# A scan-and-feed-forward kernel on one core: the late part of `a` loaded and scanned later, and the first steps put in another order

## The chip, the core and the metric

The kernel runs on one core of one Trainium2 chip. The metric is the device time of a run in microseconds. Five engines take part: TensorE (PE, with its weight loads as PEld), VectorE (DVE), ScalarE (ACT), GpSimd (POOL) and SyncE (SP, which here only issues transfers). ACT and POOL issue transfers too.

## The reference

```python
# attention-like part: 4 batches, 8 heads, 768 positions in chunks of 32, D = 32, N = 16
cum = np.cumsum(log_a[chunk]);  L = exp(cum[i] - cum[j]) for j <= i
y = (C B^T * L) x + (C state) * exp(cum)
state = exp(sum(log_a)) * state + sum_j B x * exp(cum[-1] - cum)
# feed-forward part, on the 3072 rows of 256 values that y gives
out = relu(y @ w_in) ** 2 @ w_out          # w_in 256 x 2048, w_out 2048 x 256
```

What the decay needs of `a` is the running product of `a` within chunks; everything else is products of matrices.

## The kernel before, in words

The positions are cut into 12 **units** of 256 rows: four batches for each third `j` of the sequence (units 0 to 3 have `j` = 0, units 4 to 7 `j` = 1, units 8 to 11 `j` = 2). A unit's first half makes its part of y (the tile `T`), its second half, the **block** of the same number, is the feed-forward part. In a block there are eight pairs of 128 hidden columns. For each pair, four matmuls with `w_in` (`mm1`, L390) fill one bank of PSUM, ACT evicts it with a relu into `hb` (L395), DVE squares it into `h` (L401), and four matmuls with `w_out` (`mm2`, L417) add it to the block's output.

Nothing schedules this at run time. The string `ORDER` is a list of steps, and each engine carries out its own instructions strictly in the order in which the steps stand. A step is a short token:

- `a0` to `a7` are the `mm1` steps of block 0 with their evictions, `b0` to `b7` those of block 1, and so on to `l`; `A0` to `L7` are the `mm2` steps; `qa0` squares what `a0` left. `a5@6` means that the step writes PSUM bank 6.
- `fa0`, `fa1` load the first third of `a` (32 rows of 128 values each, L117, tile `a_nat64`), and `la` loads the **late part** of it, the other two thirds (128 rows of 128 values, L544, tile `a_nat128`). `ldB1:s` loads B of unit 1 on SP's queue, `:a` stands for ACT's, and `:h`, `:l` for halves by head. `wi0` to `wi3` and `wo0` to `wo3` load quarters of `w_in` and `w_out` on POOL's queue (L141, L145).
- `sk` clips and scans the first third of `a` on DVE (L455, L456, tile `cp64`); `sp` turns it into P, the running products with positions on partitions, by small fp32 matmuls (L439). `sn` is the scan of the late part (`cp128`), `p` its matmuls (L439 again, eight of them, with a copy by ACT into `P_sb`, L525), `pn` a small product by DVE (`pick_p128`, L520), and `pt` two matmuls with it (L529, with a copy by ACT into `Ptot`, L530). Only units 4 to 11, and the carry from the first third to the second, need what the late part gives.
- For a unit: `pc`, `pb`, `px` scale or cast its C, B and x (`px` is L179); `tr` transposes on PE, `tc` copies the result; `mt` makes the scores (L222); `mk` masks a quarter of the scores directly on DVE (L231), `sc` copies a quarter by ACT and `ms` masks the copy (L240, on POOL or DVE); `u` and `in` are the products with x (L247), `ca` the carried state; `t` copies the finished `T` out of PSUM; `us`, `sf`, `za`, `zb`, `sa`, `sb` make the state for the next chunk (`zb` is L322 or L317 on DVE, `sb` is L333 on POOL).
- `id3:512@5` is three **filler** matmuls of 512 columns on constants (L463). They compute nothing and wait for nothing but their bank.

Transfers issued by SP and ACT share eight completion semaphores in turn, so each such transfer is issued only when the one eight places ahead of it in the program has landed.

Steps from unit 6 on (`rg6` and later) follow a regular pattern, in which PE always has a next step at hand.

Of the kernel before, what the change touches and what calls it, by code (L numbers as in the profile page):

```python
# [30 lines left out]
def kernel(  # L31
# [22 lines left out]
        us1 a3@7 qa2 b0@5 jz2:p qa1 b2@4 qa3 qa0 b3@6 pb2:a b1@2 qb0 ldB3:s ldC3:s pc2:v wo1 qb1 qb2 a4@7 a5@0 wi3
        b4@3 qa5 tr2@41 B0 A0 tc2:1:a iv:32:64 iv:16:32 qb3 qa4 tc2:0:a b5@5 zb1 B1 A1 mt2 B2 ldx3:s B3 A3 sc2 A2 qb4
        qb5 mk2 mk2 b7@0 wo2 ms2:v sb1 mk2 qb7 a6@5 a7@4 pb3:a wo3 px2 ld4 b6@2 A4 A5 pc3:v qa6 u2@45 ina2 inb2 tr3@31
        B5 B4 zb0 sb0 qa7 ld6 sf2 tc3:1:v qb6 pc4:p tc3:0:a ca2 pb4:p px3:v pq t2:aa us2 A6 mt3 u3@45 mk3 us3 A7 mk3
        tr4 c0@4 za3 mk3 ld5 c6@0 c5@7 B6 sa3 mk3 pc5:p afC2 pb5 c1@2 ld7 qc0 px5:p px4:v qc1 zb2 qc6 qc5 c2@4 B7 c7@1
# [679 lines left out]
```

## Time and profile before

| what | us |
|---|---|
| median of the 3 timed runs | 115.52 |
| lowest and highest of them | 115.5, 116.46 |
| profiled execution, span from first to last instruction | 114.5 |
| PE busy in it | 108.4 |
| DVE, ACT, POOL busy | 86.0, 76.6, 47.7 |

The profile is of one execution of its own; its span is 1.02 us below the median of the timed runs, which count what lies around the span as well. PE's busy time contains fillers, and it counts overlapping ends of matmuls, so a busy PE need not be doing useful work at its best rate. For that, the starts of the matmuls in the trace are the better guide.

### The profile page before, as it was taken

To read this page: it belongs to the slowest core of one execution; us is meant where nothing else is said; L and a number is where in the kernel's file an instruction comes from. 1 tells how busy PE (TensorE), PEld (TensorE's weight loads), DVE (VectorE), ACT (ScalarE), POOL (GpSimd) and SP (SyncE) were. 2 spreads that over 40 slices of the span, in tenths; PEclk is the share of its full clock that TensorE was granted. 3 is DMA by queue.
4 is the path that set the end of the run, shared out by engine and by line. 5 is a ranking of instruction groups with operands and counts; after the bars stand their busy time and mean duration, and the time that the engine had idled before them with its cause. 6 is when DMAs were issued, how large, how long until landed. Compare 5 with 4: busy or idle time off the path is not lost.

```text
span 114.5 us, 4010 instructions
## 1 busy us (share of the span) xinstructions
PE 108.4 (95%) x1629; PEld 93.8 (82%) x1630; DVE 86.0 (75%) x193; ACT 76.6 (67%) x160; POOL 47.7 (42%) x97
## 2 busy tenths in 40 slices
...
GB/s 25 204 184 165 201 188 218 214 171 175 140 166 193 86 250 105 162 95 155 156 121 134 127 97 149 104 121 51 0 98 68 0 100 0 17 80 0 92 0 92
DMA packets 47814, 13.46 MB, mean 118 GB/s; under 512 B 44276, under 2 KB 45876, under 8 KB 47796
## 3 DMA queue, kind: packets, MB, share of 16 engines
...
q0 software_dynamic: 1664, 2.10, 11.1%
q10 hardware_dynamic: 2304, 0.48, 2.0%
...
q14 instruction: 6, 0.05, 0.1%
HBM read 10.58 MB, written 3.15 MB: 120 GB/s over the span
## 4 chain that ended last, share of the span: by engine, by line
PE 77%; DMA 8%; DVE 5%; ACT 4%; issue 1%; POOL 1%; ACTq 1%; POOLq 0%
PE pp L417 33%; PE pp L390 33%; PE pp L247 7%; DMA w_out_b<-in_moe_w_out_dram 5%; PE pp L222 3%; DMA B_nat<-in_B_dram 3%; ACT hb L395 2%; DVE mts L240 1%; DVE h L401 1%; PE pp L463 1%; ACT jt L170 1%; DVE Pinv L537 1%; DVE mts L231 1%; ACT T L210 1%; POOL Sd L333 1%
## 5 line engine op out<-in xcount | busy, mean ns | idle before, releaser
L395 ACT ACTIVATE hb<-pp 128x512 bf16<-128x512 f32 x96 | 54.9, 600 | 22.5 <-PE pp L390 20.7
L401 DVE TENSOR_TENSOR h<-hb 128x512 bf16<-128x512 bf16 x96 | 44.9, 487 | 12.7 <-ACT hb L395 12.4
L417 PE MATMUL pp<-w_out_b,h 128*128 128x256 bf16 (+1 forms) x400 | 54.0, 268 | 0.1
L390 PE MATMUL pp<-T,w_in_b 128*128 128x256 bf16 x384 | 53.5, 273 | 0.1
L390 PEld LDWEIGHTS <-w_in_b 128*128 128x128 bf16 x384 | 41.5, 114 | 2.1 <-issue 0.8
L417 PEld LDWEIGHTS <-h 128*128 128x128 bf16 x400 | 37.5, 98 | 4.7 <-issue 0.9
L231 DVE TENSOR_TENSOR mts<-pp,mask 128x512 bf16<-128x512 f32 x45 | 29.7, 679 | 1.6 <-PE pp L222 1.6
L333 POOL TENSOR_TENSOR Sd<-z,Pquad 128x256 bf16<-128x256 f32 x16 | 11.0, 695 | 34.7 <-DVE z L317 22.8
L179 POOL TENSOR_TENSOR xs<-x_nat,Pinv 128x256 bf16<-128x256 f32 (+1 forms) x17 | 13.3, 800 | 2.3 <-DMA x_nat<-in_x_dram 2.2
L160 POOL TENSOR_TENSOR jt<-C_nat,P_sb 128x128 bf16<-128x128 f32 x18 | 7.9, 457 | 4.7 <-DMA C_nat<-in_C_dram 4.7
L463 PE MATMUL pp<-const-bfloat16-1.0 128*128 128x512 bf16 (+2 forms) x25 | 6.8, 427 | 1.0 <-PEq L722 0.8
L317 DVE SCALAR_TENSOR_TENSOR z<-z,Ptot,us 128x64 f32<-128x64 f32 x8 | 2.9, 356 | 5.4 <-ACT us L301 5.4
L247 PE MATMUL pp<-mts,xs 64*32 64x128 bf16 x384 | 6.1, 219 | 0.8 <-DVE mts L240 0.8
L424 ACT COPY osb<-pp 128x512 f32<-128x512 f32 x11 | 6.4, 584 | 0.5 <-PE pp L417 0.4
L172 POOL CAST jt<-B_nat 128x128 bf16<-128x128 f32 x17 | 5.5, 352 | 1.7 <-DMA B_nat<-in_B_dram 1.7
L463 PEld LDWEIGHTS <-const-bfloat16-1.0 128*128 128x128 bf16 x26 | 2.7, 116 | 3.9 <-issue 3.5
L222 PE MATMUL pp<-bct 32*64 32x256 bf16 x192 | 5.1, 280 | 0.5 <-DVE bct L212 0.5
L247 PEld LDWEIGHTS <-xs 64*32 64x32 bf16 x384 | 4.2, 90 | 1.2 <-issue 1.1
L284 ACT CAST T<-pp 128x512 bf16<-128x512 f32 x7 | 4.1, 585 | 1.6 <-PE pp L247 1.4
L210 ACT CAST T<-pp 128x256 bf16<-128x256 f32 x8 | 2.7, 375 | 2.4 <-PE pp L247 2.3
L247 PE MATMUL pp<-bct,Sd 128*128 128x128 bf16 x40 | 4.2, 220 | 0.0
...
## 6 DMA issues: line engine op xcount, KB each, us to landing
x_nat<-in_x_dram SPq DMA_DIRECT2D x11, 256.0 KB, 3.6
out_dram<-osb SPq DMA_DIRECT2D x11, 256.0 KB, 3.0
B_nat<-in_B_dram SPq DMA_DIRECT2D x11, 128.0 KB, 3.0
C_nat<-in_C_dram SPq DMA_DIRECT2D x11, 128.0 KB, 4.2
w_in_b<-in_moe_w_in_dram POOLq DMA_DIRECT2D x4, 256.0 KB, 6.6
w_out_b<-in_moe_w_out_dram POOLq DMA_DIRECT2D x4, 256.0 KB, 6.7
x_nat<-in_x_dram ACTq DMA_DIRECT2D x2, 128.0 KB, 3.5
bct<-jt SPq DMA_TRANSPOSE x8, 3.2
```

The lines of the kernel that those rows point to most:

```text
L160: eng.tensor_tensor(out=_fap(jt[k % 3], 128 + 144 * g, [[384, 2], [32, 4], [1, 16]]), in0=_fap(loaded[k]["C"], 128 * g, [[16, 2], [32, 4], ...
L179: eng.tensor_tensor(out=_fap(xs, 256 * r, [[256, 2 // n], [32, 8], [1, 32]]), in0=_fap(loaded[k]["x"], 32 * r, [[32, 2 // n], [64, 8], [1, ...
L222: nc.tensor.matmul(pp[64 * u:64 * u + 64, q, r * 256:r * 256 + 256], bct[32 * q:32 * q + 32, r, 0, u * 64:u * 64 + 64], _fap(bct[32 * q:32 ...
L231: nc.vector.tensor_tensor(out=live[k]["mts"][:, q].rearrange("p r g i -> p (r g i)"), in0=pp[:, q, :], in1=mask, op=ALU.mult)
L247: nc.tensor.matmul(dst, w, v, start=bool(need), stop=False, skip_group_check=True, **({} if pos is None else {"tile_position": pos}))
L333: nc.gpsimd.tensor_tensor(out=_fap(S_d, 0, [[128, 2], [32, 4], [1, 32]]), in0=_fap(z, 0, [[32, 2], [0, 4], [1, 32]]), in1=_fap(Pquad, 4 * ...
L390: nc.tensor.matmul(pp[:, h, i * 256:(i + 1) * 256], _fap(w, g * w.shape[2] + (o // 2) * 512 + 2 * (o % 2) + i, [[4, 128]]), T[blk][:, g].r ...
L395: nc.scalar.activation(out=hb.rearrange("p i t -> p (i t)"), in_=pp[:, h, :], func=AF.Relu)
L401: nc.vector.tensor_tensor(out=h2, in0=hb, in1=hb, op=ALU.mult)
L417: nc.tensor.matmul(dst, h2[:, i, r * 128:(r + 1) * 128], w_out_b[gi][:, 2 * o + i, c0:c1], start=first, stop=(fp == 7 and i == 1), skip_gr ...
L424: nc.scalar.copy(out=osb, in_=pp[:, 6 if blk == 1 else 7, :])
L463: nc.tensor.matmul(pp[:, h, 0:int(cols)], ones_b[:, 0:128], ones_b[:, 0:int(cols)] if dep is None else dep, start=True, stop=True, skip_gr ...
```

## The change

Only the string `ORDER` differs, and in it only the steps up to the sixth unit (to about `D0` and `e0`). The late part of `a` (`la`) moves from second place in the list to a place behind the loads of units 0 and 1; its scan (`sn`), its matmuls (`p`, `pt`) and its small product (`pn`) move behind the first `mm1` steps of blocks 0 and 1. Around that, most steps of the first six units stand in another order, some change engine (`px0` goes from POOL to DVE, `pbh0` from ACT to POOL), `mm1` and `mm2` steps of blocks 0 to 3 are exchanged among themselves, and the fillers have other numbers and sizes. The computation is the same. The core of the diff:

```diff
-        id3:512@5 fa1:a la fa0:s ku ef ldx0:h:a eb id2:512@5 ti id1:512@5 gB3 pi ldB0:l:a hd ldC0:l:a ldB0:h:s
...
-        mk1 mk1 px1:p mk1 t0:aa p2@0 a1@5 id3:128@0 a0@4 u1@12 mk1 ldC2:s ina1 inb1 pn sf1 a2@3 ca1 pt@6 t1:vv ldx2:s
...
+        jz1:v ti pi ku ldx0:h:a ldC0:h:s fa1:a ef ldC0:l:a mb hd gB3 fa0:s ldB0:l:a id2:256@3 ldx0:l:a ldB0:h:s eb
...
+        inb1 pb2:a a2@0 sf1 wo1 ca1 ldx2:s t1:vv ldB3:s a3@4 qa0 wi3 us1 sn1 qa2 qa1 b0@5 b1@7 qa3 b2@1 qb2 p2@5 pc2:p
+        qb0 pn pt@5 a5@6 ldC3:s qb1 b3@3 b4@2 qb4 a4@0 tr2@41 iv:32:64 B0 qb3 wo2 tc2:1:a B1 A0 tc2:0:v b5@2 zb1 B2 B3
```

**SP's queue at the start.** These are the first transfers that SP issues; `a_nat128` is the late part of `a`, `a_nat64` the first third, the digit in `B_nat1` is the unit. Before:

```order
L544 DMA a_nat128_98<-in_a_dram 128x1x128
L117 DMA a_nat64_97<-in_a_dram 32x128
L127 DMA B_nat0_146<-in_B_dram 128x4x32
L127 DMA C_nat0_149<-in_C_dram 128x4x32
L127 DMA B_nat1_159<-in_B_dram 128x8x32
L127 DMA C_nat1_177<-in_C_dram 128x8x32
L127 DMA x_nat1_270<-in_x_dram 128x8x64
```

And with the change:

```order
L127 DMA C_nat0_134<-in_C_dram 128x4x32
L117 DMA a_nat64_97<-in_a_dram 32x128
L127 DMA B_nat0_144<-in_B_dram 128x4x32
L127 DMA B_nat1_159<-in_B_dram 128x8x32
L127 DMA C_nat1_163<-in_C_dram 128x8x32
L127 DMA x_nat1_184<-in_x_dram 128x8x64
L544 DMA a_nat128_98<-in_a_dram 128x1x128
```

The late part went from first to seventh place, and a half of C of unit 0 stands first instead.

**PE around the matmuls of the late part.** Before, the eight matmuls of `p` (L439) stood between unit 0's carried state (`Sd0_0`) and block 0's first `mm1` step:

```order
L247 LDWEIGHTS Sd0_0_267
L247 MATMUL pp_120<-bct0_191,Sd0_0_267 128x128
L439 MATMUL pp_120<-eye_f_88,cp128_102 64x64 x4
L390 LDWEIGHTS w_in_b0_112
L390 MATMUL pp_120<-T0_334,w_in_b0_112 128x256
```

and `pt` (L529) stood between unit 1's carried state and the fourth `mm1` step of block 0. Now both stand next to each other, behind the `mm1` steps `b0`, `b1`, `b2` of block 1 (the rows with `T1`) and ahead of `a5` (the rows with `T0` and `w_in_b2`):

```order
L390 LDWEIGHTS w_in_b1_113
L390 MATMUL pp_120<-T1_436,w_in_b1_113 128x256
L439 MATMUL pp_120<-eye_f_88,cp128_102 64x64 x4
L529 MATMUL pp_120<-pick_p128_104,spread_96 128x16
L390 LDWEIGHTS w_in_b2_114
L390 MATMUL pp_120<-T0_345,w_in_b2_114 128x256
```

Before, `p` wrote bank 0 and `pt` bank 6; now both write bank 5.

**DVE around the small product of the late part.** `pick_p128` (L520) is what `pt` multiplies; `h20_2` is the square of block 0, pair 2, and `h21_0` that of block 1, pair 0. Before:

```order
L231 TENSOR_TENSOR mts1_292<-pp_120,mask_90 128x512 x4
L520 TENSOR_SCALAR pick_p128_104<-pick_94,cp128_102 128x16
L345 TENSOR_TENSOR Sd1_0_409<-pp_120,Pquad_108 128x256
L212 CAST T1_421<-pp_120 128x4x64 x2
L401 TENSOR_TENSOR h20_2_434<-hb0_2_415 128x512
```

And with the change:

```order
L456 SCALAR_TENSOR_TENSOR cp128_102<-a_cl128_100,const-float32-0.0 128x128
L401 TENSOR_TENSOR h20_2_453<-hb0_2_427 128x512
L401 TENSOR_TENSOR h20_1_455<-hb0_1_364 128x512
L401 TENSOR_TENSOR h20_3_469<-hb0_3_444 128x512
L401 TENSOR_TENSOR h21_2_477<-hb1_2_475 128x512
L401 TENSOR_TENSOR h21_0_486<-hb1_0_461 128x512
L520 TENSOR_SCALAR pick_p128_104<-pick_94,cp128_102 128x16
```

The product moved from ahead of the first squares to a place behind five of them, two of which (`h21_2`, `h21_0`) belong to block 1.

More of the change, by code (lines that the diff above doesn't have):

```diff
@@ L54 @@
[L54 to L58, printed above, removed]
@@ L69 @@
[L69 to L71 removed]
+        jz1:v ti pi ku ldx0:h:a ldC0:h:s fa1:a ef ldC0:l:a mb hd gB3 fa0:s ldB0:l:a id2:256@3 ldx0:l:a ldB0:h:s eb
+        id3:128@5 id1:512@5 jz0:v pbh0:p id2:512@5 ldB1:s sk ldC1:s id8:192@0 pbl0:p wi0 pk sp wi1 wm ldx1:s pc0:v
@@ new lines @@
+        iv1:0:8 trC0@36 px0:v ps tcC0:1:a trB0@7 tcC0:0:v tcB0:2:a id1:256@0 su id13:128@2 mt0 to u0@67 pb1:a sc0 mk0
+        sc0 id1:128@4 fq pc1:p mk0 iv:8:16 wo0 ms0:p id5:128@5 la sf0 tr1@41 px1:p iv:16:32 tc1:0:a ms0:v tc1:1:a
+        id3:512@3 us0 mt1 ldB2:s in0 ca0 t0:aa ldC2:s wi2 mk1 jz2:p mk1 mk1 id3:512@4 id2:128@4 a1@5 a0@0 u1@12 ina1 mk1
+        inb1 pb2:a a2@0 sf1 wo1 ca1 ldx2:s t1:vv ldB3:s a3@4 qa0 wi3 us1 sn1 qa2 qa1 b0@5 b1@7 qa3 b2@1 qb2 p2@5 pc2:p
+        qb0 pn pt@5 a5@6 ldC3:s qb1 b3@3 b4@2 qb4 a4@0 tr2@41 iv:32:64 B0 qb3 wo2 tc2:1:a B1 A0 tc2:0:v b5@2 zb1 B2 B3
@@ new lines @@
+        mt2 A1 sb1 A3 qa5 sc2 b7@0 qa4 ldx3:s mk2 mk2 qb5 a7@4 zb0 px2 A2 b6@2 a6@1 A5 wo3 qb7 u2@45 ms2:v pb3:p ina2
+        pc3:p sb0 mk2 ld4 inb2 qa7 tr3@20 B4 sf2 qb6 tc3:0:v afC2 ld6 tc3:1:a pb4:p qa6 px3:v A4 pc4:p ca2 B5 t2:aa A6
+        mt3 us2 tr4 mk3 u3@45 us3 ld5 za3 A7 mk3 mk3 sa3 c1@5 c6@0 mk3 pc5:p c0@4 B6 c5@7 pb5 tr5 qc6 c2@2 B7 ld7 c4@0
+        qc0 pb6:v qc5 qc2 c7@4 C0 qc1 c3@3 C5 px4:v qc4 qc7 pq zb2 rg4@56 C2 C6 mk4 mk4 mk4 qc3 d1@5 za4 d7@4 C4 qd7 mk4
+        sa4 px5:p d2@2 px6 C1 qd2 d6@4 d0@0 qd6 qd0 d3@2 d4@3 d5@1 C3 C7 qd5 qd4 rg5@45 zb4 mk5 mk5 qd1 mk5 iv:64:96 D0
```

27 lines of the change are left out of this document (11 added, 16 removed).

## The prediction

> **What bounds the kernel now.** I read the busy times first, then the chain of waits, then PE's part of the timeline. The page gives
>
> ```profile
> PE 108.4 (95%) x1629; PEld 93.8 (82%) x1630; DVE 86.0 (75%) x193; ACT 76.6 (67%) x160; POOL 47.7 (42%) x97
> ```
>
> and the busy times by stretches (PE's first, then PEld, DVE, ACT, POOL) show that PE is full soon after 15 us:
>
> ```profile
> 16.00:18.00 2.00, 2.00 (x20) 1.85 (x19) 1.90 (x7) 1.97 (x7) 0.00 (x0) 1.00 1.21 210
> ```
>
> The chain of waits (start, length, what) has these links at the places that decide:
>
> ```profile
> 1.71 3.54 DMA B_nat<-in_B_dram
> ...
> 10.54 1.36 DVE mts L240
> ...
> 12.67 0.39 ACT T L210
> 13.10 0.60 PE pp L390 x4
> ...
> 23.16 5.72 DMA w_out_b<-in_moe_w_out_dram
> 28.93 0.60 PE pp L417 x4
> ```
>
> Up to 13.10 us the kernel is a chain of short dependent steps. It ends in the masking of unit 0's scores (L240), unit 0's products, the copy of `T`, and the first `mm1` step at 13.10. I call this moment A. From there on PE always has a next step, except for the wait for the last quarter of `w_out` ahead of 28.93. So the time is A, plus PE's work behind A, plus the holes in it. An edit counts if it moves A, adds PE work behind A, or opens a hole there. All my moments are in the time of the profiled span, 114.5 us; the median of the timed runs is 115.52, 1.02 more, and I add the sum to that median.
>
> **Part 1: what A gains.** Rows of the start (transfers with kilobytes and us to landing):
>
> ```profile
> 1.23 0.45 ACTq L127 DMA_DIRECT2D x_nat<-in_x_dram  x1
> ...
> 0.81 0.74 SPq L544 DMA_DIRECT2D a_nat<-in_a_dram  x1
> 1.60 0.42 SPq L117 DMA_DIRECT2D a_nat<-in_a_dram  x1
> ...
> a_nat<-in_a_dram SPq DMA_DIRECT2D x1, 16.0 KB, 3.1
> ...
> a_nat<-in_a_dram ACTq DMA_DIRECT2D x1, 16.0 KB, 1.6
> ...
> 4.84 0.22 DVE L455 TENSOR_SCALAR a_cl<-a_nat 64x128 f32<-64x128 f32 x1 [1.16 <-DMA a_nat<-in_a_dram]
> ```
>
> The first scan waits for the half of `a` that SP issues at 1.60, behind the late part, and that lands 3.1 later, at 4.7. With the change both halves are second in their queues, issued at about 1.25 (0.81 and the 0.45 that a transfer of x or C ahead takes to issue). With the same 3.1 they land at 4.35, and the scan starts 0.35 earlier. Bounds: behind a transfer of 64 or 128 KB they may take as long as the x half did (below), 3.8, a loss of 0.2; with 1.6 they would land at 2.9, but then the halves of B and C hold the chain (one landed at 5.25, the link at 1.71 above), a gain of about 0.9 at most.
>
> ```profile
> x_nat<-in_x_dram ACTq DMA_DIRECT2D x1, 128.0 KB, 3.8
> ```
>
> The scan is not all, since the end of the chain, the masked quarter on DVE, also depends on POOL:
>
> ```profile
> 8.66 1.29 DVE L231 TENSOR_TENSOR mts<-pp,mask 128x512 bf16<-128x512 f32 x2 [0.19 <-PE pp L222]
> 10.46 1.43 DVE L240 TENSOR_TENSOR mts<-sc,mask 128x512 bf16<-128x512 bf16 x1
> ...
> 24.60 0.52 DVE L240 TENSOR_TENSOR mts<-sc,mask 128x512 bf16<-128x512 bf16 x1
> ...
> 8.84 0.76 POOL L160 TENSOR_TENSOR jt<-C_nat,P_sb 128x128 bf16<-128x128 f32 x2
> 9.56 1.14 POOL L240 TENSOR_TENSOR mts<-sc,mask 128x512 bf16<-128x512 bf16 x1
> 10.65 0.76 POOL L141 DMA_DIRECT2D w_in_b<-in_moe_w_in_dram  x1
> 11.41 0.57 POOL L145 DMA_DIRECT2D w_out_b<-in_moe_w_out_dram  x1
> ```
>
> The same operation took 0.52 at 24.60 and 1.43 at 10.46, where POOL was in its own masking until 10.7 and in a weight issue until 11.41: DVE's ended 0.48 behind that issue. It waited for POOL. [...]
>
> In the change POOL issues `wo0` (0.57, as at 11.41) between unit 1's C and its masking, and no longer scales unit 0's x. I put POOL's masking at about 9.75 to 10.9. DVE has two masks, two reciprocals and the state ahead of its quarter, where it had two masks, the state and a copy; it arrives 0.35 earlier than 10.46, at 10.1, waits, and ends near 11.45 instead of 11.89. That is a gain of 0.45 for A, with the earlier scan in it, since POOL's unit 1 work waits for the landing of C, which hardly moves. Bounds: DVE goes first, 10.1 + 0.52, a gain of 1.2; or POOL's scaling of unit 1's x (1.07) also goes ahead, a loss of 0.65. I take **-0.45**, nearest to the order in which both stand; A' = 12.65.
>
> **Part 2: what the scan's late place adds.** Before, `p` and `pt` cost PE nothing:
>
> ```profile
> 12.55 0.46 PE L439 MATMUL pp<-eye_f,cp 128*64 128x64 f32 x8
> 13.10 0.60 PE L390 MATMUL pp<-T,w_in_b 128*128 128x256 bf16 x4
> ...
> 15.51 0.35 PE L529 MATMUL pp<-pick_p,spread 128*128 128x16 f32 x2
> 15.70 3.73 PE L390 MATMUL pp<-T,w_in_b 128*128 128x256 bf16 x32
> ```
>
> `p` ran while PE waited for `T` of unit 0, `pt` while the copy of `T` of unit 1 was under way (DVE, 15.24 to 16.13, in the next rows). Now both are behind A, where PE is full. Worse, `pt` waits. Its operand `pick_p128` stands on DVE behind the squares of `b2` and `b0`, and its bank is free only when ACT has copied `p` out of it, behind the eviction of `b2`. The prices:
>
> ```profile
> 15.24 0.89 DVE L212 CAST T<-pp 128x256 bf16<-128x256 f32 x2
> 16.34 2.09 ACT L395 ACTIVATE hb<-pp 128x512 bf16<-128x512 f32 x4
> 16.11 1.95 DVE L401 TENSOR_TENSOR h<-hb 128x512 bf16<-128x512 bf16 x5
> 14.21 0.22 DVE L520 TENSOR_SCALAR pick_p<-pick,cp 128x16 f32<-128x16 f32 x1
> 22.31 1.17 DVE L401 TENSOR_TENSOR h<-hb 128x512 bf16<-128x512 bf16 x2
> ...
> 13.05 0.27 ACT L525 COPY P_sb<-pp 128x128 f32<-128x128 f32 x1
> ```
>
> An eviction costs 0.60, spaced by 0.50; a square 0.42, in a row 0.34; an `mm1` step costs PE 0.44 (32 matmuls from 15.70 in 3.73 with the last one's tail). In both kernels block 1 starts when `T1` is copied, 16.13 - 13.10 = 3.03 behind A. Three steps of 0.44 end at A' + 4.35, `p` starts its last matmul at 4.7. `b2`'s result is complete at 4.5. ACT, with evictions of `a2`, `a3`, the state copy, `b0` and `b1` ahead of it, evicts `b2` from 4.7 to 5.3. DVE squares `b2` (0.42) and `b0` (0.34) and makes `pick_p128` (0.22), so `pt` can start at 6.3, and with its 0.2 of PE time `a5` starts at A' + 6.5. In the kernel before, the step behind three steps of block 1 or 0 in this place starts at A + 4.35. The difference is **+2.15**: 0.35 for `p`, 1.6 of hole, 0.2 for `pt`. ACT's copies of P are ready at 5.6 and don't decide. Queued behind `pt` on PE is everything, and behind `Ptot`'s copy on ACT the eviction of `a5`. Bounds: if ACT had no backlog 0.2 less, 1.95; if DVE's squares were held by POOL as one was (two in 1.17 at 22.31), 2.5. Nothing later gives this back, since PE had no hole there to lose.
>
> **Part 3: the last quarter of `w_out`.** Its issue waits on POOL behind a state that waits for DVE's `z`:
>
> ```profile
> 22.12 0.28 DVE L322 SCALAR_TENSOR_TENSOR z<-us,Ptot 128x64 f32<-128x64 f32 x1
> 22.54 0.66 POOL L333 TENSOR_TENSOR Sd<-z,Pquad 128x256 bf16<-128x256 f32 x1 [7.02 <-DVE z L322]
> 23.16 0.60 POOL L145 DMA_DIRECT2D w_out_b<-in_moe_w_out_dram  x1
> 23.77 1.07 POOL L179 TENSOR_TENSOR xs<-x_nat,Pinv 128x512 bf16<-128x512 f32 x1
> ```
>
> PE was ready for `A6` at 28.56 and got it at 28.93, a hole of 0.37. Now `xs` (1.07) stands ahead of this issue too. Behind `pt` the `z` comes at about A' + 10.2, the state at 10.5, `xs` at 11.1, the issue at 12.15, the landing 5.72 later at 17.9; PE arrives at A' + 17.7 (28.56 - 13.10 + 0.1 + 2.15). The hole shrinks to about 0.2: **-0.15**, bounds -0.4 (gone) and +0.6 (a landing as slow as 6.7, a row below).
>
> The rest I cost at nothing: the order of `mm1` and `mm2` steps of blocks 0 to 3 leaves PE's work the same, and behind 29 us PE has no hole in the kernel before that a better order could fill. Its cover is PE's own queue; a step that came too early would open a hole of one eviction and one square, about 1 us.
>
> **Sum:** -0.45 + 2.15 - 0.15 = +1.55, that is 114.5 + 1.55 = 116.05 for the span and 115.52 + 1.55 = **117.1 us** for the median. With the bounds of the parts the sum runs from +0.35 (115.9) to +3.75 (119.3).
>
> **Rivals.** *DVE goes first (not slower).* If DVE's masked quarter is ready before POOL starts its own, it takes 0.52 at once, A moves by 1.2, and with the hole of part 3 gone the sum is -1.2 + 1.95 - 0.4 = +0.35: **115.9**. For it speaks that POOL has more issues ahead of its masking; against it that DVE has one reciprocal more. From a gain of 0.85 at A on, the kernel is within 1% of before.
>
> *The weights hold PE instead.* The third quarter of `w_in` stood at 10.65 and took 6.7:
>
> ```profile
> w_in_b<-in_moe_w_in_dram POOLq DMA_DIRECT2D x1, 256.0 KB, 6.7
> ...
> w_in_b<-in_moe_w_in_dram POOLq DMA_DIRECT2D x1, 256.0 KB, 7.7
> ```
>
> Now it is behind unit 1's x, at about 12.5, and lands at 19.2, just when `a5` needs it (A' + 6.5 = 19.15). With the fourth quarter's 7.7 it lands at 20.2 and adds 1.05: **118.1**. The hole in part 2 hides this wait, so the two don't add up unless the landing is later still.
>
> *PE's clock stays slow.* The fillers show two rates:
>
> ```profile
> 0.85 4.71 PE L463 MATMUL pp<-const-bfloat16-1.0 128*128 128x512 bf16 x11 [0.85 <-PEq L722]
> 8.74 1.03 PE L463 MATMUL pp<-const-bfloat16-1.0 128*128 128x512 bf16 x4 [0.16 <-issue]
> ```
>
> 0.43 each at the start, about 0.22 apart later. In the change the fillers ahead of the first scan have 3968 columns instead of 5632, at the first rate 3.3 us instead of 4.7, and then PE waits more than 1 us. If the faster rate isn't reached there, the 13 small fillers ahead of unit 0's scores cost 0.7 more and the three ahead of A 0.6, and each us of dense work at half rate costs 0.5 until the rate changes: +1.3 to +3.5 on the sum, **119.5** in the middle. Against it: PE is not idle for long anywhere. [...]
>
> That the change doesn't do what it says I leave out: the order of the instructions shows it.
>
> **How the numbers follow.** Forecast 0.52, DVE first 0.23, weights 0.14, slow clock 0.11. A measurement of this kernel can tell about 1%, 1.16 us, from no change. The forecast's own range is 116.5 to 117.7, mostly above 116.7, so of its 0.52 I count 0.47 as slower; weights and clock are slower, 0.25; of "DVE first" 0.05 is faster, 0.17 the same and 0.01 slower. Faster 0.05, same 0.22, slower 0.73. The range, 115.8 to 119.3, leaves out the faster tail and half of the slow clock.
>
> **What would show it.** Right: in the profile after, the first scan starts before 4.7; the first `mm1` step lies between 12.0 and 13.0; two L439 and L529 groups stand among the `mm1` steps with a PE hole of 1.3 to 1.9 us between them, ended by DVE's `pick_p`; `a5` starts 6.5 behind A. Wrong: a hole under 1 us there, a first `mm1` before 12, PE filler spacing of 0.11 for 128 columns (slow clock), or a wait for `w_in_b` that ends behind `pt`.

## The result, and the profile after

| what | before | after |
|---|---|---|
| median of the timed runs, one chip | 115.99 (4 runs) | 118.8 (4 runs) |
| lowest and highest | 115.5, 116.94 | 118.43, 120.08 |
| profiled execution, span | 114.5 | 117.0 |

The ratio is 1.029, with a 95% interval of 1.020 to 1.037. So the change is slower by 3.3 us, 2.9% of the 115.5 that the forecast started from; the medians in the table differ by 2.8, the two profiles by 2.5. The forecast was slower by 1.55, 117.1. Ratios compare undisturbed runs alone (only five of the twelve of the first kernel of experiment 10), and where few of these were left the text gives spans instead.

The page of after, busy times and the granted clock in 40 slices:

```profile
PE 109.7 (94%) x1648; PEld 96.0 (82%) x1648; DVE 86.3 (74%) x191; ACT 76.5 (65%) x158; POOL 50.1 (43%) x101
PEclk9976999999999999999999999999999999999999
```

The clock row read 9 (90% or more) in every slice before. Now slices 3 and 4, 6 to 12 us, are lower. The busy times by stretches (PE's first, then PEld, DVE, ACT, POOL, granted clock) say the same, and show the hole at 18 to 20 us, where PE is busy for 0.51 of 2:

```profile
6.00:8.00 2.00, 2.00 (x30) 1.63 (x37) 1.00 (x3) 1.29 (x6) 1.62 (x5) 0.82 0.81 160
8.00:10.00 2.00, 2.00 (x45) 1.53 (x45) 1.32 (x3) 1.13 (x3) 1.44 (x3) 0.50 1.25 193
...
18.00:20.00 2.00, 0.51 (x5) 0.54 (x6) 1.23 (x4) 0.67 (x3) 0.00 (x0) 1.00 1.30 211
```

PE's part of the timeline (start, length, what):

```profile
4.99 0.43 PE L439 MATMUL pp<-eye_f,cp 64*64 64x32 f32 x8 [0.82 <-POOL jt L172]
...
6.81 1.20 PE L463 MATMUL pp<-const-bfloat16-1.0 128*128 128x128 bf16 x13
7.94 0.65 PE L222 MATMUL pp<-bct 32*64 32x256 bf16 x16
...
13.04 1.03 PE L390 MATMUL pp<-T,w_in_b 128*128 128x256 bf16 x8
...
17.44 0.46 PE L439 MATMUL pp<-eye_f,cp 128*64 128x64 f32 x8
19.49 0.36 PE L529 MATMUL pp<-pick_p,spread 128*128 128x16 f32 x2 [1.59 <-DVE pick_p L520]
19.71 1.91 PE L390 MATMUL pp<-T,w_in_b 128*128 128x256 bf16 x16
...
28.52 0.61 PE L247 MATMUL pp<-mts,xs 64*32 64x128 bf16 x17
29.52 0.40 PE L247 MATMUL pp<-mts,xs 64*32 64x128 bf16 x15 [0.39 <-DVE mts L231]
29.86 0.51 PE L197 MATMUL pp<-eye_b,jt 128*128 128x128 bf16 x6
...
38.72 0.51 PE L247 MATMUL pp<-mts,xs 64*32 64x128 bf16 x32
```

DVE and POOL of after, in order of time:

```profile
4.17 0.22 DVE L455 TENSOR_SCALAR a_cl<-a_nat 64x128 f32<-64x128 f32 x1
9.32 1.15 POOL L240 TENSOR_TENSOR mts<-sc,mask 128x512 bf16<-128x512 bf16 x1 [0.56 <-ACT sc L236]
10.44 1.04 POOL L179 TENSOR_TENSOR xs<-x_nat,Pinv 128x512 bf16<-128x512 f32 x1
10.58 1.18 DVE L240 TENSOR_TENSOR mts<-sc,mask 128x512 bf16<-128x512 bf16 x1
...
18.44 0.76 DVE L401 TENSOR_TENSOR h<-hb 128x512 bf16<-128x512 bf16 x2 [0.54 <-ACT hb L395]
19.12 0.23 DVE L520 TENSOR_SCALAR pick_p<-pick,cp 128x16 f32<-128x16 f32 x1
...
28.00 0.87 DVE L240 TENSOR_TENSOR mts<-sc,mask 128x512 bf16<-128x512 bf16 x1
28.79 0.68 DVE L231 TENSOR_TENSOR mts<-pp,mask 128x512 bf16<-128x512 f32 x1
```

The first scan starts 0.67 earlier (4.17 against 4.84), but unit 0's scores (L222) only 0.2 earlier (7.94 against 8.15), and A (the first `mm1` step) comes at 13.04, where it stood at 13.10. The hole stands where it was forecast. A second wait, ahead of 29.52, was not forecast. The products of unit 2 take from 28.52 to 29.86, 1.34, where they took 0.51 (26.78 to 27.29) before.

**The kernel before, profiled again.** Its timed runs have spans of mostly 113 to 115, with medians of 113.4 to 114.2 on four chips; the first profile's 114.5 is on the late side. So the unchanged kernel was profiled once more.

> The kernel before, unchanged, profiled once more. The timed runs of it have spans of 112.9 to 115.6, mostly 113.2 to 114.2, and its profile, at 114.5, is among the later ones. Theory (the length of DVE's masked quarter L240, 1.43 in that profile and 0.53 with the scan taken away, differs from execution to execution): this execution has a span near 113.5, L240 near 0.5 and the first `mm1` step near 12.1; with a span near 114.5, L240 is again above 1.2. Rival (the spread comes from somewhere else): L240 and the first `mm1` step stay at 1.4 and 13.1 whatever the span.

```profile
10.15 1.43 DVE L240 TENSOR_TENSOR mts<-sc,mask 128x512 bf16<-128x512 bf16 x1
...
12.79 0.60 PE L390 MATMUL pp<-T,w_in_b 128*128 128x256 bf16 x4
...
15.39 3.73 PE L390 MATMUL pp<-T,w_in_b 128*128 128x256 bf16 x32
...
35.40 0.51 PE L247 MATMUL pp<-mts,xs 64*32 64x128 bf16 x32
```

The span is 113.7. L240 is long again, so its length does not explain why the spans of the kernel before spread; what is earlier is the head by 0.3, and the wait for `w_out` ahead of 28.93 is not there. With this profile the account closes. The mark "unit 4" is the start of unit 4's products (36.01 in the first profile of before), and the last column is a kernel that is told below:

| stretch, us | before, 1st | before, 2nd | after | mended |
|---|---|---|---|---|
| start to A | 13.10 | 12.79 | 13.04 | 11.89 |
| A to `a5` or the step in its place | 4.35 | 4.35 | 6.67 | 5.34 |
| from there to unit 4 | 18.56 | 18.26 | 19.01 | 18.20 |
| unit 4 to the end | 78.5 | 78.3 | 78.3 | 78.4 |
| span | 114.5 | 113.7 | 117.0 | 113.8 |

Against the second profile the change costs 0.25 + 2.32 + 0.75 = 3.3, what the timed runs show. Nothing comes from behind unit 4.

### The profile page after: what moved, and what is told of

Read it like the earlier page. It is cut to its first block, busy times and chain, and to the rows that moved or that the text cites. A ratio compares the mean times of both kernels' runs of the same rounds, so it can differ in the third digit from the quotient of the medians.

```text
span 117.0 us, 4048 instructions
## 1 busy us (share of the span) xinstructions
PE 109.7 (94%) x1648; PEld 96.0 (82%) x1648; DVE 86.3 (74%) x191; ACT 76.5 (65%) x158; POOL 50.1 (43%) x101
## 4 chain that ended last, share of the span: by engine, by line
PE 83%; DVE 7%; DMA 2%; ACT 2%; issue 1%; SPq 1%; POOL 0%; ACTq 0%; POOLq 0%
PE pp L417 35%; PE pp L390 33%; PE pp L247 6%; PE pp L222 4%; DVE mts L231 3%; PE pp L463 3%; DMA B_nat<-in_B_dram 2%; DVE h L401 2%; PE pp L197 2%; ACT hb L395 2%; DVE mts L240 1%; SPq L117 0%; SPq L127 0%; PE pp L439 0%; DVE T L212 0%
## 5 line engine op out<-in xcount | busy, mean ns | idle before, releaser
L401 DVE TENSOR_TENSOR h<-hb 128x512 bf16<-128x512 bf16 x96 | 45.8, 495 | 13.6 <-ACT hb L395 13.4
L231 DVE TENSOR_TENSOR mts<-pp,mask 128x512 bf16<-128x512 f32 x45 | 29.6, 681 | 3.8 <-PE pp L222 3.8
L333 POOL TENSOR_TENSOR Sd<-z,Pquad 128x256 bf16<-128x256 f32 x16 | 11.9, 752 | 37.8 <-DVE z L317 27.9
L179 POOL TENSOR_TENSOR xs<-x_nat,Pinv 128x256 bf16<-128x256 f32 (+1 forms) x16 | 12.5, 802 | 0.0
L160 POOL TENSOR_TENSOR jt<-C_nat,P_sb 128x128 bf16<-128x128 f32 x22 | 9.4, 443 | 1.6 <-DMA C_nat<-in_C_dram 1.6
L463 PE MATMUL pp<-const-bfloat16-1.0 128*128 128x128 bf16 (+3 forms) x44 | 7.7, 341 | 0.8 <-PEq L722 0.8
L247 PE MATMUL pp<-mts,xs 64*32 64x128 bf16 x384 | 6.6, 219 | 0.5 <-DVE mts L231 0.4
L463 PEld LDWEIGHTS <-const-bfloat16-1.0 128*128 128x128 bf16 x44 | 4.6, 129 | 2.6 <-issue 1.9
L172 POOL CAST jt<-B_nat 128x128 bf16<-128x128 f32 x18 | 6.1, 365 | 1.2 <-DMA B_nat<-in_B_dram 1.0
L222 PE MATMUL pp<-bct 32*64 32x256 bf16 x192 | 5.3, 291 | 0.0
```

What stands on the lines that cost most here:

```text
L160: eng.tensor_tensor(out=_fap(jt[k % 3], 128 + 144 * g, [[384, 2], [32, 4], [1, 16]]), in0=_fap(loaded[k]["C"], 128 * g, [[16, 2], [32, 4], ...
L179: eng.tensor_tensor(out=_fap(xs, 256 * r, [[256, 2 // n], [32, 8], [1, 32]]), in0=_fap(loaded[k]["x"], 32 * r, [[32, 2 // n], [64, 8], [1, ...
L222: nc.tensor.matmul(pp[64 * u:64 * u + 64, q, r * 256:r * 256 + 256], bct[32 * q:32 * q + 32, r, 0, u * 64:u * 64 + 64], _fap(bct[32 * q:32 ...
L231: nc.vector.tensor_tensor(out=live[k]["mts"][:, q].rearrange("p r g i -> p (r g i)"), in0=pp[:, q, :], in1=mask, op=ALU.mult)
L247: nc.tensor.matmul(dst, w, v, start=bool(need), stop=False, skip_group_check=True, **({} if pos is None else {"tile_position": pos}))
L333: nc.gpsimd.tensor_tensor(out=_fap(S_d, 0, [[128, 2], [32, 4], [1, 32]]), in0=_fap(z, 0, [[32, 2], [0, 4], [1, 32]]), in1=_fap(Pquad, 4 * ...
```

## The experiments

**The changed kernel, profiled again**, to see what varies in it.

> The changed kernel, unchanged, profiled once more. Theory (PE's rate in the head differs from execution to execution, since its fillers end at 4.2): unit 0's scores start between 7.5 and 9.0, at 9.0 with the matmuls of P at 0.64 and thirteen fillers in 1.57, at 7.5 with 0.43 and 0.93; the span is 116.5 to 118.4, with the hole ahead of `pt` between 1.5 and 1.9 in any case. Rival (the head is the same, and what varies stands behind it): the scores start at 7.9 again.

The span was 118.5. The scores started at 7.85, A was at 12.95 and the hole 1.90. The head was the same as in the first profile; the extra time lies behind the hole, where the 16 matmuls of the next four steps took 2.83 instead of 1.91 and the six transposes (L197) behind them 0.85 instead of 0.50; the granted clock over the whole span was 0.971, 0.983 in the first profile. The theory on the head failed for this execution.

**1. `pn` early, `pt` in another bank.**

```diff
-us1 sn1 qa2
+us1 sn1 pn qa2
...
-qb0 pn pt@5 a5@6
+qb0 pt@2 a5@6
```

> The changed kernel, with the small product `pn` directly behind the late scan on DVE (ahead of the squares) and `pt` in bank 2 instead of bank 5. Theory (the order on DVE makes the hole): `pt` no longer waits for two squares nor for the copy of `p`; it starts behind `p`, at about 17.9 instead of 19.49, `a5` at about 18.1 instead of 19.71, and the span falls by about 1.6 from the 117.0 of the changed kernel to 115.4; the median falls from 118.8 to about 117.2. Rival one (the third quarter of `w_in` lands late): its issue stood at 11.43 and took up to 7.6, so `a5` starts at about 19.0 and only 0.7 is gained. Rival two (the loss comes from the slow clock before 12 us or from what follows behind 22 us): the hole goes, but PE waits as long a little later, and the span stays within 0.4 of 117.0.

Ratio to before 1.021 (1.015 to 1.028), span 116.9. PE:

```profile
4.84 0.64 PE L439 MATMUL pp<-eye_f,cp 64*64 64x32 f32 x8 [0.53 <-DVE warm L473]
...
7.45 1.57 PE L463 MATMUL pp<-const-bfloat16-1.0 128*128 128x128 bf16 x13
8.95 0.65 PE L222 MATMUL pp<-bct 32*64 32x256 bf16 x16
...
14.46 1.03 PE L390 MATMUL pp<-T,w_in_b 128*128 128x256 bf16 x8
...
19.25 0.40 PE L529 MATMUL pp<-pick_p,spread 128*128 128x16 f32 x2
19.50 1.94 PE L390 MATMUL pp<-T,w_in_b 128*128 128x256 bf16 x16
```

The hole is gone: `a5` starts 5.04 behind A instead of 6.67, a gain of 1.63. But in this execution the head was slower. The matmuls ahead of 13 us took up to twice as long as in the first profile of before (0.64 for those of P, 0.43 there; 0.50 for a filler of 512 columns in place of 0.26), so A came at 14.46, and the profile shows next to no gain. The ratio fell from 1.029 to 1.021. The lowest span of the six runs, 115.4 against 116.7 in after's, hints at a gain of 1.3, but that run left no profile.

**2. The early fillers as long as before.**

```diff
-id2:256@3
+id2:512@3
...
-id3:128@5
+id2:512@5
...
-id8:192@0
+id2:512@0
...
-pk sp wi1
+pk sp id7:192@0 wi1
```

> The changed kernel, with nine fillers of 512 columns ahead of the first matmuls of P in the place of the shorter ones, and seven more of 192 columns behind them, as the kernel before had. Theory (the clock is a small part): the granted clock reads 1.00 from 6 us on, the 13 fillers of 128 columns and unit 0's scores take the faster rate, the scores start at about 7.5 instead of 7.94 if the seven new fillers do not hold them, the first `mm1` step comes 0.3 to 0.5 earlier, and the span falls by at most 0.5 from 117.0. Rival (the slow clock is the main loss): a fall of 1.3 or more, to 115.7 or less. Third possibility: no change at all, because POOL's masking of unit 0, not PE, sets the first `mm1` step.

Ratio 1.023 (1.017 to 1.030), span 116.8. PE:

```profile
6.76 0.93 PE L463 MATMUL pp<-const-bfloat16-1.0 128*128 128x128 bf16 x13
7.62 0.42 PE L222 MATMUL pp<-bct 32*64 32x256 bf16 x16
...
12.49 1.04 PE L390 MATMUL pp<-T,w_in_b 128*128 128x256 bf16 x8
...
19.26 0.37 PE L529 MATMUL pp<-pick_p,spread 128*128 128x16 f32 x2 [1.91 <-DVE pick_p L520]
```

A comes 0.55 earlier, a little more than expected, and the hole is 0.3 longer, so less than half of it is left at the end. POOL and DVE ahead of A:

```profile
9.89 1.04 POOL L179 TENSOR_TENSOR xs<-x_nat,Pinv 128x512 bf16<-128x512 f32 x1
10.03 1.18 DVE L240 TENSOR_TENSOR mts<-sc,mask 128x512 bf16<-128x512 bf16 x1
```

L240 takes as long beside POOL's scaling of x as in after (1.18); with PE's rate up (unit 0's scores take 0.42, in after 0.65), all of it happens 0.55 earlier. A stands 0.16 from the 12.65 of the prediction, though not for the prediction's reason.

**3. Both together.**

> The changed kernel with both edits: the long early fillers, and `pn` directly behind the late scan with `pt` in bank 2. Theory (two separate losses, PE's slow rate in the head and the hole ahead of `pt`): each edit by itself left the other loss in place. Together the first `mm1` step starts at about 12.5, `a5` 5.0 behind it at about 17.5, against 13.04 and 19.71 in the changed kernel, and the span falls by 2.2 to about 114.8. Rival (something later, a weight, unit 2's masks or a buffer, bounds the first 30 us whatever stands ahead of it): the span stays at 116 or more.

Ratio 1.018 (1.011 to 1.026), span 115.5. A was at 12.93 (the matmuls of P took 0.64 again, the scores 0.42), `a5` at 18.06, 5.13 behind it. In this execution PE's rate rose late, so A gained only 0.11 against after, and the gain is that of the hole. By the ratios, the edits take off 0.8% and 0.5% alone and 1.1% together; the intervals overlap, so whether the two add up is not shown. The span expected was 0.7 less.

**4. The fillers alone, in the kernel before.**

```diff
-id3:512@5 fa1:a
+id2:256@5 fa1:a
...
-id3:512@5 sk pbh0:a id2:512@5 pk
+id1:512@5 sk pbh0:a id1:512@5 id8:192@0 pk
...
-id7:192@0 px0:p
+px0:p
```

One more line, not shown, cuts two of 512 columns to three of 128.

> The kernel before, with the early fillers cut to the changed kernel's 3968 columns, and without the seven of 192 columns behind the matmuls of P; all else as before. Theory (PE falls back to its slow rate when it has no fillers between about 4.2 and 6 us): the matmuls of P, the transposes, unit 0's scores and the five fillers of 512 columns behind them run at the slow rate (0.64, 0.65 and 0.43 each instead of 0.43, 0.42 and 0.22), the first `mm1` step comes 0.4 to 1.4 later, and the span is 114.9 to 115.9 against 114.5, with a wide spread from run to run. Rival (the rate of PE in the head doesn't matter, since POOL and DVE set the first `mm1` step): within 0.3 of the kernel before.

Ratio 1.014 (1.007 to 1.021). PE, and then the granted clock by stretches:

```profile
5.50 0.64 PE L439 MATMUL pp<-eye_f,cp 64*64 64x32 f32 x8 [1.19 <-POOL jt L172]
...
8.61 2.31 PE L463 MATMUL pp<-const-bfloat16-1.0 128*128 128x512 bf16 x5
...
14.72 1.04 PE L390 MATMUL pp<-T,w_in_b 128*128 128x256 bf16 x4
```

```profile
8.00:10.00 2.00, 2.00 (x36) 0.76 (x21) 1.40 (x4) 1.52 (x5) 1.88 (x5) 1.00 1.13 187
```

The lengths were as the theory had them: the fillers end at 4.3, PE waits 1.19, and then takes 0.64 for the matmuls of P, 0.66 for unit 0's scores and 2.31 for five fillers (0.43, 0.42 and 1.27 in the second profile of before), up to the first `mm1` step (1.04 where four took 0.60). That PE fell back from a faster rate is not shown. The time at A was not as expected: A comes 1.6 later than in the first profile of before and 1.9 later than in the second, where 0.4 to 1.4 was expected. This execution took 116.8, the four that the ratio counts 114.7 to 116.5, so the usual price at A is probably smaller than 1.9. The granted clock reads 1.00 all the while.

When PE's rate rose differed from run to run. With the long early fillers and those behind the matmuls of P, as the kernel before and experiments 2, 3 and 5 to 7 have them, it rose before 6.6 us in every profile: the matmuls of P took 0.43 there, or, where they took 0.64 (experiments 3 and 5), the transposes that start at 6.34 and 6.59 took 0.50, not the 0.85 to 0.92 of the slow rate. With the short fillers, from 0.85 to between 4.1 and 4.4, it varied. In both profiles of after it was up at 5 us (0.43 for the matmuls of P, behind a wait of 0.82 or 0.78) and fell again behind 7 (the granted clock was 0.82 and 0.77 in 6 to 8 us and 0.50 in 8 to 10 us in both), behind one more wait of 0.38. In the others it rose only near 9.5 (the first kernel of experiment 9), 13 (experiment 1) or 16 (here): equal products went from 0.31 to 0.25 by 9.52, from 0.40 to 0.29 by 13.57, and from 0.31 to 0.25 by 16.65.

**5. POOL: the issue of `wi2` ahead of the scaling of x**, added to experiment 3.

```diff
-tr1@41 px1:p iv:16:32
+tr1@41 wi2 px1:p iv:16:32
...
-ldC2:s wi2 mk1
+ldC2:s mk1
```

> The same with, on POOL, the issue of the third quarter of `w_in` ahead of unit 1's scaling of x instead of behind it. Theory (DVE's masked quarter L240 waits for POOL's tensor instructions, not for its issues): POOL is in its issue from 9.89 to 10.65 when DVE comes to L240 at 10.03, so L240 takes 0.5 instead of 1.18, and the first `mm1` step comes 0.5 to 0.6 earlier than in the kernel with the two edits alone; the span falls by as much, to about 114.2. Rival (the issue holds DVE as long as a tensor instruction does, as it seemed in the kernel before, where L240 ended at 11.89, 0.48 behind an issue): L240 takes 0.9 to 1.2, and 0 to 0.3 is gained.

Ratio 1.011 (1.006 to 1.017), span 115.1. DVE and POOL:

```profile
10.56 0.76 POOL L141 DMA_DIRECT2D w_in_b<-in_moe_w_in_dram  x1
10.72 0.36 DVE L240 TENSOR_TENSOR mts<-sc,mask 128x512 bf16<-128x512 bf16 x1
```

L240 takes 0.36 beside the issue, where it took 1.18 beside the scaling. From unit 0's scores (8.31) to A (12.53) it is now 4.22, 4.87 in experiment 3: a gain of 0.65. That is what the theory expected of L240; the span fell by 0.4, where 0.5 to 0.6 was expected. L240's 1.43 in the kernel before, beside two issues of weights, does not fit the theory and stays open.

**6. Unit 2's masks**, added to 5: the last square of block 1 behind them.

```diff
-wo3 qb7 u2@45 ms2:v pb3:p ina2 pc3:p sb0 mk2 ld4
+wo3 u2@45 ms2:v pb3:p ina2 pc3:p sb0 mk2 qb7 ld4
```

> The kernel of the edit before this one, with the square of block 1's last pair behind unit 2's last masks on DVE instead of ahead of them. Theory (the hole of 0.4 ahead of the end of unit 2's products is DVE's order): the masks end 1.0 earlier, the hole of 0.4 goes, and the span falls by 0.4, to about 113.8, if the square is still ahead of its `mm2` step. Rival (DVE is the bound there, whatever its order): the hole turns up at the next `mm2` step, and nothing is gained.

Ratio 1.007 (1.003 to 1.011), span 114.7, A at 11.79. Unit 2's products took 1.06 (26.00 to 27.06) instead of 1.34, and a wait of 0.21 for a square came up behind them. So the order on DVE was one part of it. A was at 12.53 in experiment 5; that it is earlier here comes from PE's rate, which was up at the matmuls of P (0.43, there 0.64), not from the edit.

**7. The mended kernel:** 6 with the cast of unit 3's B on ACT, as the kernel before has it.

```diff
-mk2 mk2 qb5 a7@4 zb0
+mk2 mk2 qb5 a7@4 pb3:a zb0
...
-ms2:v pb3:p ina2
+ms2:v ina2
```

> The changed kernel with all edits that helped and the group still late: the long early fillers, `pn` early and `pt` in bank 2, the third quarter of `w_in` ahead of unit 1's scaling of x, the last square of block 1 behind unit 2's masks, and the cast of unit 3's B by ACT. Theory (unit 2's wait of 0.33 comes from POOL's casts, as in the run where it went with the cast on ACT): the span is 0.3 below that of the same kernel with the cast on POOL, 114.0 to 114.3, and what is left against the kernel before is `p`, `pt` and their gaps on PE, 0.75, less what is gained at the first `mm1` step. Rival (the cast on ACT delays evictions by as much): no change.

Ratio 1.0003 (0.996 to 1.004), span 113.8. PE, then DVE:

```profile
11.89 1.04 PE L390 MATMUL pp<-T,w_in_b 128*128 128x256 bf16 x8
...
16.77 0.40 PE L529 MATMUL pp<-pick_p,spread 128*128 128x16 f32 x2
17.23 1.94 PE L390 MATMUL pp<-T,w_in_b 128*128 128x256 bf16 x16
...
26.07 0.57 PE L247 MATMUL pp<-mts,xs 64*32 64x128 bf16 x32
26.58 0.51 PE L197 MATMUL pp<-eye_b,jt 128*128 128x128 bf16 x6
```

```profile
24.65 0.41 DVE L240 TENSOR_TENSOR mts<-sc,mask 128x512 bf16<-128x512 bf16 x1
```

L240 took 0.41, unit 2's products 0.51 as in the kernel before, and the whole loss is gone, with the load, the scan, `p` and `pt` still in their late places. What these cost on PE (5.34 against 4.35) is about what A gains (11.89 against 12.79). That the cast is what held L240 at unit 2 is not shown by this alone: here L240 fell into a pause of POOL (24.64 to 24.81), and in the third kernel of experiment 9, with the same cast on ACT, it took 1.21.

**8. The group's place by itself, in the kernel before.**

```diff
-sc0 pc1:p sn1 mk0
+sc0 pc1:p mk0
...
-t0:aa p2@0 a1@5
+t0:aa a1@5
...
-inb1 pn sf1 a2@3 ca1 pt@6 t1:vv ldx2:s us1 a3@7
+inb1 sf1 a2@3 ca1 t1:vv ldx2:s us1 sn1 a3@7
...
-qa0 b3@6 pb2:a b1@2 qb0
+qa0 b3@6 qb2 p2@5 pb2:a qb0 pn pt@5 b1@2
...
-qb1 qb2 a4@7
+qb1 a4@7
```

> The kernel before, with only the late group moved: scan, `p`, `pn` and `pt` stand where the change has them, behind the first steps of block 1, `p` and `pt` in one bank, `pn` behind the squares; the late part of `a` is loaded first as before. Theory: a hole of 1.3 to 1.8 us ends at `pt`, PE is behind by 2.0 to 2.4 from there on, and the span is 116.5 to 116.9 against 114.5; the median is 1.8 to 2.1 per cent above the kernel before. The scan's 0.9 us fall out of DVE's time ahead of 8.66 and enter behind 16, which by itself costs nothing there. Rival (the loss of the change needs its other edits, the fillers, the loads or the order of the blocks' steps): under 1.0 per cent.

Ratio 1.012 (1.006 to 1.017), span 115.4. DVE, then PE:

```profile
10.17 0.53 DVE L240 TENSOR_TENSOR mts<-sc,mask 128x512 bf16<-128x512 bf16 x1
```

```profile
11.91 0.60 PE L390 MATMUL pp<-T,w_in_b 128*128 128x256 bf16 x4 [0.53 <-ACT T L210]
...
18.13 0.37 PE L529 MATMUL pp<-pick_p,spread 128*128 128x16 f32 x2 [1.06 <-ACT jt L170]
18.34 1.91 PE L390 MATMUL pp<-T,w_in_b 128*128 128x256 bf16 x16
```

The step behind `pt` starts 6.43 behind A, 2.08 more than before: the term was as forecast. The hole of 1.06 is put down to ACT's `jt`, but `pick_p` ended at 17.99, 0.14 ahead of `pt`, as in after. Against the first profile of before the span rose by 0.9 only, because A came 1.2 earlier (1.7 and 0.9 against the second); L240 took 0.53 instead of 1.43.

**9. The group back near its old place, in the changed kernel.** First with the scan ahead of L240, `p` ahead of the first `mm1` step, `pn` and `pt` as before (all four taken out where they stood):

```diff
-iv:16:32 tc1:0:a ms0:v
+iv:16:32 tc1:0:a sn1 ms0:v
...
-id3:512@4 id2:128@4 a1@5
+p2@7 id1:512@4 id2:128@4 a1@5
...
-inb1 pb2:a a2@0 sf1 wo1 ca1 ldx2:s
+inb1 pn pb2:a a2@0 sf1 wo1 ca1 pt@6 ldx2:s
```

> The changed kernel, with the late part still loaded late, but its scan ahead of DVE's masked quarter, `p` ahead of the first `mm1` step (bank 7, in the place of two fillers of 512 columns), `pn` behind unit 1's masks and `pt` behind unit 1's carried state (bank 6), so near the places of the kernel before. Theory (the place of the group costs 2.3): `p` and `pt` cost PE nothing again, the first `mm1` step stays at 13.0, the step `a5` starts at about 17.4 instead of 19.71, the span falls to about 114.7, within 0.4 of the kernel before's 114.5. Rival one (weights): `a5` waits for the third quarter of `w_in` until about 19.0, and the span is about 116.3. Rival two (slow clock and the rest of the order make the loss): the span stays above 116.5.

Then the same on top of 6, with the scan behind L240; then with the cast of 7 as well; and once with the late part loaded ahead of unit 1's B (`la ldB1:s`), scan ahead of unit 0's masks.

> The changed kernel with the long early fillers, the third quarter of `w_in` ahead of unit 1's scaling of x, the last square of block 1 behind unit 2's masks, and the late part of `a` loaded late as in the change; but its scan directly behind unit 0's masked quarter L240 on DVE, `p` ahead of the first `mm1` step, `pn` behind unit 1's masks and `pt` behind unit 1's carried state. Theory (the late place of `p` and `pt` still costs 0.75 when there is no hole): the first `mm1` step stays at 11.8, `a5` follows 4.4 behind it instead of 5.12, and the span is 113.8 to 114.2, against 114.3 to 114.7 for the kernel with the group late. Rival (the scan delays unit 1's masks and the copy of its `T` by as much as is gained): no change.

> The kernel of the run before this one, with the cast of unit 3's B by ACT instead of POOL, as the kernel before has it. Theory (POOL's back-to-back instructions hold DVE's L240 at unit 2, 1.22 against 0.52): L240 takes 0.5 to 0.8 there, the wait of 0.33 of unit 2's products goes, and the span falls by 0.3. Rival (DVE's own queue makes the masks late): L240 is short and the wait stays.

> The changed kernel with the long early fillers, the third quarter of `w_in` issued ahead of unit 1's scaling of x, and the last square of block 1 behind unit 2's masks, and now with the late group near its place in the kernel before: the late part of `a` loaded behind unit 0's loads but ahead of unit 1's, its scan in DVE's idle time ahead of unit 0's masks (about 7 us), `p` ahead of the first `mm1` step in the place of two fillers, `pn` behind unit 1's masks, `pt` behind unit 1's carried state. Theory (what is left of the late place is PE's own time for `p` and `pt`, 0.75 with what goes around them, since `a5` stood 5.12 behind the first `mm1` step without a hole, against 4.35 in the kernel before): `a5` comes 4.4 behind the first `mm1` step, which stays at about 11.8, and the span is about 113.9 against 114.7. Rival (as in the first try with the group moved back, the scan or the late landing holds unit 0's masks): the first `mm1` step comes later than 12.3, and nothing is gained.

Ratios 1.039 (1.034 to 1.043), 1.022 (1.018 to 1.026) and 1.021 (1.017 to 1.026) for the first three; none brought what was expected. The theory was right on the distance (`a5` 4.26 behind A in the first), but A itself moved: 15.28 in the first, 14.15 in the second, 14.01 in the third. In the first, PE's rate rose late as in experiment 1 (0.64 for the matmuls of P, scores at 8.94), and L240 stood behind the clip, which took 0.98, and the scan, so that PE waited 1.04 for it. `a5` stood at 19.54 even so, 0.17 ahead of after; what made its span 118.4 were waits of 1.43 for L240 and 0.39 for L231 at unit 2. In the second, SP and DVE:

```profile
5.67 0.72 SPq L544 DMA_DIRECT2D a_nat<-in_a_dram  x1
...
11.95 0.86 DVE L455 TENSOR_SCALAR a_cl<-a_nat 128x128 f32<-128x128 f32 x1 [1.22 <-DMA a_nat<-in_a_dram]
```

The late part, issued at 5.67, landed at 11.95 only, and then the clip took 0.86 beside POOL (0.22 elsewhere). So `p` waited for 1.84. In the third the part was there by 10.66, but the clip took 2.00 beside POOL's scaling and the memset behind it, and `p` waited for 1.84 again; unit 2's products had no wait, as expected, though L240 still took 1.21. In the fourth the part, issued at 3.55, was scanned at 7.28, in time. One of its six spans was 114.2, near the 113.9 expected, the others 118.4 to 120.4; in the profile, of 120.4, it was unit 1's C that came late:

```profile
4.81 0.58 SPq L127 DMA_DIRECT2D C_nat<-in_C_dram  x1
...
11.81 0.76 POOL L160 TENSOR_TENSOR jt<-C_nat,P_sb 128x128 bf16<-128x128 f32 x2 [3.86 <-DMA C_nat<-in_C_dram]
```

So none of the four has the late load and the old place of the group together without a loss at A, by the landing in the second, by the clip's length in the first and third, and by C in the fourth. That it can't be done is not shown.

**10. The kernel before with the scan behind L240**, and the same with the late part loaded behind unit 1's C and one early filler less.

```diff
-sc0 pc1:p sn1 mk0 mk0
+sc0 pc1:p mk0 mk0
...
-ldx1:s ms0:v tc1:0:a
+ldx1:s ms0:v sn1 tc1:0:a
```

The second one's further lines:

```diff
-fa1:a la fa0:s
+fa1:a fa0:s
...
-id2:512@5 pk pbl0:p
+id1:512@5 pk pbl0:p
...
-sp ldC1:s iv1:0:8
+sp ldC1:s la iv1:0:8
```

> The kernel before, with one step moved: the scan of the late part stands behind unit 0's masked quarter L240 on DVE instead of ahead of unit 0's masks. Theory (without the scan ahead of it DVE comes to L240 in time, as in the run with the whole group late, where it took 0.53 instead of 1.43): the first `mm1` step stands at 11.9 to 12.2 instead of 12.79 and 13.10 in the two profiles of the kernel before, the scan fits ahead of `p`, and the span falls by 0.5 to 0.9, to 113.0 to 113.3. Rival (the length of L240 is a matter of which engine happens to get through first): 1.4 again, and no change.

> As the kernel before with the scan behind L240, and besides the late part of `a` loaded behind unit 1's C instead of first, with one early filler of 512 columns less. Theory (the late load lets the first scan start earlier, the one thing that the change's own idea gains): the first scan starts at 4.2 to 4.4 instead of 4.84, the matmuls of P 0.2 to 0.5 earlier than 5.5, and the first `mm1` step and the span as much earlier as the run before this one. Rival (the halves of B and their casts, or unit 1's C behind more transfers, hold the chain as before): within 0.15 of the run before this one, or later.

Ratios 1.0005 (0.995 to 1.006) and 1.038 (1.033 to 1.043). In the first, L240 took 0.54, as its theory had it, but the scan behind it took 1.21 (0.42 elsewhere). The mask behind the scan then came late, `p` waited 1.33 for it, and A was at 13.23. In the second the scan of the first third started at 3.60, 1.2 earlier, but L240 took 1.43 again, and the late part's clip 2.02 behind it; A was at 15.10. The late load does bring the first scan forward; nothing of that reaches A.

**11. The kernel before without L240 on DVE.** The last quarter is masked from PSUM (L231).

```diff
-tr1@41 sc0 ms0:p sf0 tc1:1:v ldx1:s ms0:v tc1:0:a
+tr1@41 mk0 ms0:p sf0 tc1:1:v ldx1:s tc1:0:a
```

> The kernel before, with unit 0's last quarter of scores masked by DVE directly from PSUM (L231, 0.6) instead of a copy by ACT and the masking of the copy (L240, 0.53 or 1.43 there). Theory (L240 needs something that POOL's masking holds, L231 does not): the quarter is masked by about 10.6 beside POOL's own until 10.5, the products of unit 0 end at about 11.1, and the first `mm1` step starts at 11.9 to 12.1 in place of 12.79 and 13.10; the span is 112.9 to 113.4, the ratio to the kernel before 0.992 to 0.998. Rival (what holds DVE there is something else, or the end of unit 0's products is set by POOL's masking): the first `mm1` step stays at 12.8.

Ratio 1.006 (1.002 to 1.010). The three masks took 1.89 in a row, in part beside POOL's own masking, and three in the kernel before 1.87, but the copy behind them then came late for unit 1's scores (a wait of 1.08 on PE). A was at 12.58, not at 12, and the time did not fall.

A kernel with all of unit 2's masks made from PSUM is left aside: its step `b7` wrote bank 0 before the first quarter was masked, so it computes something else. No version beats the kernel before by more than the measurement can tell.

## Why the prediction was right, and where it was wrong

The direction was right and the size was not: 1.55 forecast, 3.3 measured. Against the second profile of before, part 1 misses by 0.70, part 2 by 0.17, and part 3 with the rest that I cost at nothing by 0.90: 1.77 in all.

**What bounds the kernel:** right. A, PE's work behind it and the holes add up to the span in the four profiles of the table.

**Part 1, the gain at A:** wrong. The scan came 0.67 earlier (0.35 forecast), but A gained 0.06 against the first profile of before and lost 0.25 against the second, where -0.45 was forecast. Two steps failed. The first made most of the miss: PE's rate stood in the sum at nothing, and only in a rival with a chance of 0.11. It was part of the result, 0.55 at A by experiment 2, and in the kernel before 1.4% by the fillers alone. The second is what DVE waits for. I had L240 wait for POOL's masking and end near 11.45; that masking ended at 10.47, 0.43 earlier than I had put it, and POOL's scaling of x followed at once, beside which L240 took until 11.76. The case of my bound of +0.65 came about, but not its size, since the masking was earlier. The 0.65 of experiment 5 is the same number by chance. In experiment 2, L240 stood beside the scaling too, and A still came within 0.16 of the forecast 12.65: there the forecast of A met by luck. My reading of the 1.43 in the kernel before, as a wait for the issue that ends at 11.41, is not settled either, since POOL was then in a second issue until 11.98. That L240 waits for the end of an instruction of POOL was my reading of 1.43 against 0.52, and the runs do not settle it: L240 took 1.18 beside POOL's scaling (after, experiment 2), 0.36 beside an issue (experiment 5) and 0.53 with the same offsets to POOL's work as in before (experiment 8).

**Part 2, the group's late place:** right. 2.32 against 2.15 forecast; a hole of 1.59, ended by `pick_p`, against 1.6. Experiment 1 took the hole away (1.63), and what is left of the late place without it is 0.69 (5.04 against 4.35), where I had 0.55. Experiment 8 found 2.08 in the other kernel.

**Part 3, `w_out`:** the hole of 0.37 is gone, as one of the bounds had it, but the second profile of before has none either, so it was no gain to count, and 0.15 of the sum's error is from here.

**"The rest I cost at nothing":** wrong, and the largest single miss. The diff moves the cast of unit 3's B from ACT to POOL, the scaling of its C from DVE to POOL, and a square ahead of unit 2's last two masks. Unit 2's products then took 0.83 more (1.34 against 0.51). Experiment 6 gave back 0.28 and experiment 7 the remaining 0.55; why L240 was long there is open in part (experiment 7). I had named a hole "of about 1 us" as the price of a step that came too early, and had not looked for it at this place.

**The base:** the first profile of before was a late execution. Against the second the same change is 0.8 larger, and that is the rest of the way from 2.5 to 3.3.

**The rivals:** DVE did not go first. No wait for `w_in_b` ends behind `pt` in after. PE's slow rate was there in part, not at 5 us (0.43 for the matmuls of P) but from 7 us on (0.65 for the scores, granted clock 0.50 in 8 to 10 us), and I gave it too little, although the row on the fillers spoke for it.

Open: why L240 took 1.43 in both profiles of before and in the second kernel of 10, always ending 0.1 before the end of POOL's second issue, and 0.53 and 0.54 in two kernels with the same offsets to POOL's work; what held L240 at unit 2; and why the same short fillers bring PE's rate up at 5 us in one kernel and at 13 or 16 in another.
